# Unused bytes between the halves of the weights' tiles in a gated mix of linear attention and a gated unit

## The chip, the cores and the metric

The kernel runs on one core of one Trainium2 chip. The metric is the time of one execution in device microseconds (us), the median of several runs. Beside it there is one execution recorded by the hardware profiler, and all views of the profile are of that one.

## The reference

An input `x` of 2048 tokens by 640 goes through two branches, and a gate per token mixes them. Everything is float32.

```python
g = _sigmoid((x * gate_w).sum(-1, keepdims=True))
# a: linear attention, 32 heads of 20
qkv = (x @ wqkv) ...                       # q, k, v: 2048 x 640 each
phi = lambda t: jnp.where(t > 0, t + 1, jnp.exp(t)) + 1e-6
kv  = einsum("bhsd,bhse->bhde", phi(k), v);  z = einsum("bhsd->bhd", phi(k))
num = einsum("bhqd,bhde->bhqe", phi(q), kv); den = einsum("bhqd,bhd->bhq", phi(q), z) + 1e-6
a   = (num / den) @ wo
# b: gated unit, F = 1536
h = _sigmoid(x @ w_gate) * (x @ w_up)
b = h @ w_down
return g * a + (1 - g) * b
```

## The kernel before

**Precision.** Every large product is made of three matmuls (`mm3`, lines 189 to 193). Each operand is split by ScalarE and VectorE into a high part and a low part, both float32r (`split`, line 219). `mm3` issues high by high (L190), weights' high by the streamed low part (L191), and weights' low by the streamed high part (L192). So the weights loaded into TensorE go high, high, low, and each matmul loads its own 128 x 128 weights. Nearly all matmuls after the first phase stream 512 columns.

**Stages.** First K and the state (sum over tokens of phi(K) and x): 320 and 322 columns wide, tiles of many sizes. Then the tokens go in two passes of 1024: `pr` = 1, then `pr` = 0. A pass has a Q projection (`q_phase`), twelve blocks of the gated unit (`f_phase`, class `Block`) with the down-projection woven in, and `last_down`. At the end, the output stage multiplies the scaled phi(Q), `pq`, by a combined matrix held in `ws` and `wf` tiles and mixes.

**A block.** `Block.s1` to `s7` form the gate and the up product of 128 features together, with seven products in place of eight (sums of tiles are formed first). In terms, a term being one `mm3`: `s1` and `s2` use five of `wg`; `s4` one and `s6` three of `wu`; `s3`, `s4`, `s5` and `s7` two, two, two and three of `ws`. That is 18 terms, 54 matmuls. What is streamed are the forms of `x`: tiles `xa`, `xr`, `xb`, `xt`, with h or l for the part. A Q projection unit takes 15 matmuls with `wg`; of its streamed tiles those for the first two chunks of the second half are `b12`.

**Weights.** In the first pass a weights' tile is made by splitting (`wg_split`, `queue_s`) and stored to DRAM by GpSimd's queue (`store_w`, line 800). In the second pass SyncE's queue loads it back (`load_form`, line 871), two blocks ahead, into the buffer that the block before last has just left. The tiles are `wg` (two halves of 640), `wu` (two of 384) and `ws` (two of 1152 floats per partition), two buffers each; half 0 is the high part, half 1 the low part. A `wg` tile also holds the last two down weights of the second pass (`load_wd`). One `ws` and one `wu` tile serve the output stage as plain room (`load_m`, `load_p`).

**Where tiles lie.** Pools are stacked from two sides of SBUF. On the right, from the top downward: `px` (the `x` forms, later `pl` and `pq`), `pg` (`wg`), `pw` (from its bottom upward: `t`, `wu`, `ws`, `c`). All these tiles have sizes that are multiples of 256 bytes, and in the program's allocation all of them start at 224 modulo 256: `wg` at bytes 153,568 and 158,688, `wu` at 118,752 and 121,824, `ws` at 124,896 and 134,112, the `x` forms from 163,808 on. On the left lie `hf` (the products h), `wd` and `wf` (down weights): 47,456, 79,200 and 63,840, all at 96 modulo 256. At the very bottom of SBUF there are 16,384 bytes per partition that GpSimd's DMA uses as scratch. In the first phase tiles have sizes such as 2,576 and 1,288 bytes and lie at all multiples of 32 modulo 256.

**Order.** `Order` plans in program order when ScalarE's and VectorE's side work is issued between matmuls, from estimated durations; each engine and queue then runs its own list in order.

Of the kernel before, what the change touches and what calls it, by code (L numbers as in the profile page):

```python
# [8 lines left out]
F32R = mybir.dt.float32r  # L9
# [6 lines left out]
P = 128  # L16
S, D, F = 2048, 640, 1536
# [3 lines left out]
TG = 512  # L21
# [146 lines left out]
def gated_mix_kernel(ctx: ExitStack, tc: tile.TileContext, xt, xn, wk, wv, wo, wst_q, wst_f, out_t):  # L168
    nc = tc.nc
# [7 lines left out]
    def f32(ap):  # L177
        return ap.bitcast(F32)
# [40 lines left out]
    def split(hi, lo, src, after=""):  # L219
        act(hi, src, AF.Copy, after)  # L220
        at = order.act

        def low():
            order.vec = max(order.vec, at)
            vec2(lo, src, f32(hi), OP.subtract)
        order.then(low)
# [37 lines left out]
    def m1_tile(tag, name, dt=F32, rows=P):  # L264
        return m1.tile([rows, D], dt, name=name, tag=tag, bufs=2)
# [114 lines left out]
    def queue_forms(nx):  # L380

        nx[0].queue_a()
        nx[0].queue_b()
        order.add(0, 0, lambda: nx[1].load(((0, 0, 2), (0, 2, KC), (1, 2, KC), (1, 0, 2))))
        nx[1].queue_a()
        nx[1].queue_b()
        nx[1].queue_sums()
        order.add(0, 0, lambda: nx[0].load(((1, 2, 4), (0, 0, 2), (1, 0, 2), (0, 2, 4))))
        nx[0].queue_sums()
# [67 lines left out]
    def queue_ks():  # L457
        for s, sums in ((1, (0, 2, 1)), (0, ()), (2, ()), (3, (3,))):
            for j in range(2):
                for t in sums:  # L460
                    order.add(0, v_cost(HW), lambda t=t, j=j: k_sum(t, j))
            for j in range(2):
                order.add(a_cost(HW), v_cost(HW), lambda s=s, j=j: k_form(s, j), ("ks", s))
        order.add(a_cost(HW), 2 * v_cost(HW), k_fifth_d, ("ks", 5))
# [4 lines left out]
    def tok(b, side):  # L469

        pr, j = divmod(b, 4)
        return (2 * pr + side) * 4 + j
# [14 lines left out]
    def queue_xn(b):  # L487
        for n in (2 * b, 2 * b + 1):
            order.add(a_cost(D), v_cost(D), lambda n=n: split_xn(n), ("xn", b), lambda n=n: xn_st[n][1])
# [115 lines left out]
    def k_split(i, after=""):  # L605
        r = KR[i]
        ph, pl = op_tile("pkh"), op_tile("pkl")
        vh, vl = (t[:, :D].rearrange(view2, j=2) for t in (ph, pl))
        act(vh, r, AF.Copy, after, bias=EPS)
        at = order.act  # L610

        def low():
            order.vec = max(order.vec, at)
            vec3(vl, r, EPS, f32(vh), OP.add, OP.subtract)
        order.then(low)
        PK[i] = (ph, pl)
# [12 lines left out]
    def queue_split(b):  # L629
        for s in range(2):  # L630
            order.add(a_cost(D), v_cost(D), lambda s=s: k_split(tok(b, s)), ("pk", b))

    def queue_z(b):
        for s in range(2):
            order.add(0, v_cost(D), lambda s=s: z_add(tok(b, s)), ("z", b))
# [84 lines left out]
    g = GTBatch(0, [0])  # L720
# [8 lines left out]
    for c in range(1, 4):  # L729
        ck = chunks[c]  # L730
        if c == 1:
            a, b = KPlain(2), KPlain(3)
            order.need((ck, "plain"))
            queue_ks()
            queue_xn(2)
            order.need(("z", 0))
            for k in range(KC):
                a.k(k)
                order.fill()
            order.need(("z", 1))  # L740
            a.phi_a()
            for k in range(KC):
                b.k(k)
                order.fill()
                if k == 0:
                    a.phi_b()
                    order.add(0, 0.6, constants)
            order.need(("ks", 5))
            for t in range(2):
                k_split(tok(2, t))  # L750
        else:
            a, b = KBlock(2 * c), KBlock(2 * c + 1)
            for n in range(1, 6):
                order.need((ck, n))
                if c == 2 and n >= 3:
                    order.need(("ks", (1, 0, 2)[n - 3]))
                getattr(a, f"s{n}")()
                getattr(b, f"s{n}")()
                if n == 2:
                    queue_xn(2 * c)  # L760
            order.need((ck, 6))
            if c == 2:
                order.need(("ks", 5))
            if c + 1 < len(chunks):
                chunks[c + 1].load()
            else:
                nx = [Chunk(1, i, None, i * CW, xst_v, (b12h, b12l)) for i in range(2)]
                nx[0].load()
            a.s6()
            a.s7()  # L770
            order.need(("z", 2 * c - 1))
            a.sum_b()
            a.phi_a()
            b.s6()
            a.phi_b()
            order.need(("pk", 2 * c - 1))
            k_split(tok(2 * c, 0))
            b.s7()
            b.sum_b()
            k_split(tok(2 * c, 1))  # L780
        if c == 3:
            pa_cm.__exit__(None, None, None)
            px_cm = tc.tile_pool(name="px", bufs=1, side="right", reuse_waits="tile")
            px = px_cm.__enter__()
            xf = XForms(px, TG)
            pg_cm = tc.tile_pool(name="pg", bufs=1, side="right", reuse_waits="tile")
            pg = pg_cm.__enter__()
            W, WT = {}, {}

            def wg_tile():  # L790
                return pg.tile([P, 2, D], F32R, name="wg", tag="wg", bufs=2)

            def put(n, i, t):
                WT[n, i] = t
                W[n, i] = [t[:, c] for c in range(2)]

            def store_w(n, i):

                w_dram[n[2], i] = dram.tile(list(WT[n, i].shape), F32, name=f"w{n[2]}{i}")
                nc.gpsimd.dma_start(w_dram[n[2], i], f32(WT[n, i]))  # L800

            def wg_split(n, src):
                put(n, 0, wg_tile())
                split(*W[n, 0], src)
                if n[0] == "f":
                    order.then(lambda: store_w(n, 0))
            nx[0].f = nx[1].f = xf
        elif c == 1:
            chunks[2].load()
        g = GTBatch(c, batches[c])  # L810
        order.need(("xn", 2 * c))
        queue_z(2 * c)
        if c < 3:
            chunks[c + 1].queue()
        else:
            queue_xn(7)
        for u in range(4):
            g.part(u, 0, 2, ("rot", "dd", "ch", "cc")[u])
            if u == 0:
                order.need(("z", 2 * c))  # L820
                b.phi_a()
            if u == 1:
                b.phi_b()
        queue_split(2 * c + 1)
        queue_z(2 * c + 1)
        if c < 3:
            queue_xn(2 * c + 1)
        else:
            w_stage = [m1_tile("ma", "w0") for _ in range(2)]
            for n in range(2):  # L830
                nc.sync.dma_start(w_stage[n], wst_q[:, n])
            queue_forms(nx)
        for u in range(2 * KC):
            g.part(u, 2 if u < 4 else 0, 4)
            order.fill()
# [17 lines left out]
    pw = pw_cm.__enter__()  # L853
# [7 lines left out]
        return pw.tile(list(shape), dt, name=name, tag="c", bufs=5)  # L861

    def wu_tile():
        return pw.tile([P, 2, 3 * P], F32R, name="wu", tag="wu", bufs=2)

    def ws_tile():
        return pw.tile([P, 2, 9 * P], F32R, name="ws", tag="ws", bufs=2)

    def load_form(n, i):
        t = (wg_tile, wu_tile, ws_tile)[i]()  # L870
# [820 lines left out]
    PL, PQ, BL, OMG, MHL = {}, {}, {}, {}, {}  # L1691
# [7 lines left out]
    def load_m(i):  # L1699

        n = (0, 3, 10)
        t = (ws_tile, wf_tile)[i]().rearrange("p a b -> p (a b)")[:, :(n[i + 1] - n[i]) * D]
        nc.sync.dma_start(f32(t), mp_dram.rearrange("p a b c -> p (a b c)")[:, n[i] * D:n[i + 1] * D])
        for j in range(n[i], n[i + 1]):
            MHL[divmod(j, 2)] = t[:, (j - n[i]) * D:(j - n[i] + 1) * D]

    def load_p(g):

        n = groups.index(g)
        if n == 0:  # L1710
            PL[g] = [tt("pl") for _ in range(KC - 1)]
            PL[g].append(f32(wu_tile()).rearrange("p a b -> p (a b)")[:, :TG])
            for u in range(KC):
                nc.sync.dma_start(PL[g][u], p_dram[:, u, g])
        else:
            PL[g] = []
            for u in range(0, KC, 2):
                t = (x2_tile if n % 2 else h_tile)(dt=F32)
                w = min(2, KC - u)
                nc.sync.dma_start(t[:, :w], p_dram[:, u:u + w, g])  # L1720
                PL[g] += [t[:, i] for i in range(w)]
        PL[g, "at"] = order.pe + 6.0
# [137 lines left out]
```

## Time and profile before

| | |
|---|---|
| median of 3 runs | 758.25 us (757.82 to 758.86) |
| profiled execution | 760.14 us; span 758.4 us from first to last instruction |
| granted clock of TensorE | 0.999 |
| busy | TensorE 750.9 us in 3,699 matmuls, VectorE 558.3, ScalarE 309.1, GpSimd 72.9 |
| DMA | 155.27 MB, mean 205 GB/s |

The span leaves out what lies around the first and last instruction, so the profiled execution's own time stands beside it. In the rows, `PE` is TensorE's matmuls and `PEld` its weight loads, `DVE` VectorE, `ACT` ScalarE, `POOL` GpSimd, `SPq` SyncE's queue. A row of a group has the line, engine and operation, the tiles (written <- read, or for matmuls: written <- streamed, weights), the shape, the count, and then the busy time in us and the mean duration of one in ns. A row of the timeline has start and duration in us. A matmul's duration is longer than the distance to the next start, since matmuls are pipelined; differences of durations, and distances between starts, are what can be compared. A row of windows gives, for a stretch, busy us and count of each engine, the granted clock, the busy share of the DMA engines and GB/s. A row of DMA issues gives count, KB each and the median us from issue to landing.

### The profile page before, as it was taken

The page shows a single profiled execution, that of the slowest core. Times are in us where ns is not written, and L with a number is a line of the kernel's source. Part 1 is how long each engine was busy: PE and PEld are TensorE (multiplying, and loading weights), DVE is VectorE, ACT ScalarE, POOL GpSimd, SP SyncE. Part 2 cuts the span into 40 slices and gives each one's busy share as a digit, 9 for nine tenths or more (in the row PEclk, how much of TensorE's full clock was granted, in tenths as well). Part 3 has the DMA queues.
Part 4 walks back from the last instruction along what each step waited for, and adds up shares of the span by engine and source line. Part 5 has one row for each costly group of instructions (what it writes and reads, how often), then busy time and mean ns, then how long its engine had stood idle before and what let it go on. Part 6 is the DMA issues. An engine that isn't in the chain of part 4 may idle for free.

```text
span 758.4 us, 10012 instructions
## 1 busy us (share of the span) xinstructions
PE 750.9 (99%) x3699; PEld 642.3 (85%) x3699; DVE 558.3 (74%) x978; ACT 309.1 (41%) x578; POOL 72.9 (10%) x131
## 2 busy tenths in 40 slices
PE   9999999999999999999999999999999999999998
PEld 7999999988878888888888888788888888887886
DVE  4988778876586677877888865575868776886863
ACT  5673546366465634343444454353222313221110
POOL 0000000023122422121121210000000000000000
PEclk9999999999999999999999999999999999999999
DMA  7230414597987797566475744956363636277243
GB/s 260 67 109 1 140 39 135 181 276 263 334 320 267 276 380 277 207 255 241 190 258 220 288 164 148 381 200 237 124 243 132 241 119 243 91 270 257 105 139 111
DMA packets 57110, 155.27 MB, mean 205 GB/s; under 512 B 9303, under 2 KB 20823, under 8 KB 53861
## 3 DMA queue, kind: packets, MB, share of 16 engines
q1 hardware_dynamic: 44933, 99.31, 38.9%
q0 software_dynamic: 12128, 55.32, 18.8%
q8 instruction: 29, 0.48, 0.3%
q14 instruction: 20, 0.16, 0.1%
HBM read 97.33 MB, written 60.56 MB: 208 GB/s over the span
## 4 chain that ended last, share of the span: by engine, by line
PE 88%; DMA 5%; issue 2%; DVE 2%; ACT 1%; POOL 1%; SPq 1%; POOLq 0%; ACTq 0%; DVEq 0%
PE dd L192 8%; PE dd L190 8%; PE dd L191 8%; PE ch L190 8%; PE ch L192 8%; PE ch L191 8%; PE rot L191 7%; PE rot L192 7%; PE rot L190 7%; PE cc L192 6%; PE cc L190 6%; PE cc L191 6%; DMA wst<-wst_f 2%; DMA pden<-p_dram 2%; DMA wv_sb<-wv 1%
## 5 line engine op out<-in xcount | busy, mean ns | idle before, releaser
L202 ACT ACTIVATE c<-ch 128x512 f32<-128x512 f32 x72 | 43.0, 597 | 157.3 <-PE ch L192 155.6
L206 DVE TENSOR_TENSOR hf<-c,hf 128x512 fp32r<-128x512 f32 x63 | 43.2, 688 | 27.0 <-ACT hf L202 26.4
L206 DVE TENSOR_TENSOR tb<-dd,tb 128x512 f32<-128x512 f32 x75 | 51.1, 687 | 15.0 <-PE dd L192 14.6
L206 DVE TENSOR_TENSOR c<-cc,c 128x512 f32<-128x512 f32 x48 | 32.9, 685 | 29.6 <-ACT c L202 22.6
L202 ACT ACTIVATE c<-c 128x512 f32<-128x512 f32 x48 | 30.1, 628 | 49.8 <-DVE c L206 49.8
L206 DVE TENSOR_TENSOR tb<-rot,tb 128x512 f32<-128x512 f32 x64 | 43.5, 687 | 6.2 <-PE rot L192 5.8
L202 ACT ACTIVATE hf<-c 128x512 fp32r<-128x512 f32 x63 | 39.3, 625 | 18.8 <-DVE c L206 18.5
L190 PE MATMUL dd<-xrh,wg 128*128 128x512 f32 x102 | 40.0, 392 | 0.0
L191 PE MATMUL dd<-xrl,wg 128*128 128x512 f32 x102 | 39.8, 390 | 0.0
L192 PE MATMUL dd<-xrh,wg 128*128 128x512 f32 x102 | 39.7, 390 | 0.0
L190 PE MATMUL ch<-xth,ws 128*128 128x512 f32 x96 | 37.5, 390 | 1.2 <-ACT c L202 1.2
L192 PE MATMUL ch<-xth,ws 128*128 128x512 f32 x96 | 37.5, 391 | 0.0
L191 PE MATMUL ch<-xtl,ws 128*128 128x512 f32 x96 | 37.4, 389 | 0.0
L190 PE MATMUL rot<-pkh,xnh 128*128 128x320 f32 x102 | 31.6, 310 | 0.0
L191 PE MATMUL rot<-pkl,xnh 128*128 128x320 f32 x102 | 31.6, 309 | 0.0
L192 PE MATMUL rot<-pkh,xnl 128*128 128x320 f32 x102 | 31.4, 308 | 0.0
L206 DVE TENSOR_TENSOR c<-c,c 128x512 f32<-128x512 f32 x44 | 30.2, 686 | 1.4 <-ACT c L202 0.9
L1016 POOL DMA_DIRECT2D p_dram<-qr x20 | 11.1, 555 | 205.7 <-DVE qr L210 198.5
L192 PE MATMUL cc<-xbh,ws 128*128 128x512 f32 x72 | 28.0, 389 | 0.0
L190 PE MATMUL cc<-xbh,ws 128*128 128x512 f32 x72 | 28.0, 389 | 0.0
L191 PE MATMUL cc<-xbl,ws 128*128 128x512 f32 x72 | 28.0, 389 | 0.0
L202 ACT ACTIVATE pq<-pl 128x512 fp32r<-128x512 f32 x14 | 8.5, 630 | 40.3 <-DVE pl L210 40.3
(474 smaller groups left out, 2300.9 us busy)
## 6 DMA issues: line engine op xcount, KB each, us to landing
w<-ws POOLq DMA_DIRECT2D x12, 1152.0 KB, 7.1
ws<-w SPq DMA_DIRECT2D x12, 1152.0 KB, 8.5
wst<-wst_f SPq DMA_DIRECT2D x12, 640.0 KB, 5.5
w<-wg POOLq DMA_DIRECT2D x12, 640.0 KB, 4.8
wd<-wd POOLq DMA_DIRECT2D x12, 640.0 KB, 6.5
wg<-w SPq DMA_DIRECT2D x12, 640.0 KB, 4.2
xst<-xt SPq DMA_DIRECT2D x10, 640.0 KB, 6.5
wf<-wd SPq DMA_DIRECT2D x10, 640.0 KB, 5.5
```

The lines of the kernel that those rows point to most:

```text
L190: nc.tensor.matmul(out, l_hi, r_hi, start=first, stop=False, skip_group_check=True)
L191: nc.tensor.matmul(out, l_hi, r_lo, start=False, stop=False, skip_group_check=True)
L192: nc.tensor.matmul(out, l_lo, r_hi, start=False, stop=last, skip_group_check=True)
L202: nc.scalar.activation(out, src, fn, **kw)
L206: nc.vector.tensor_tensor(out, a, b, op=op)
L1016: nc.gpsimd.dma_start(p_dram[:, u, g], r)
```

## The change

Each half of a weights' tile gets unused bytes behind it: 96 for `wg`, 32 for `wu`, 64 for `ws`. The tile that the rest of the program sees is cut back to the old width, so no matmul, split or transfer changes its amount of data; in SBUF a tile that was one run per partition becomes two. The two places that use a tile as plain room take the whole of it. The scratch of GpSimd's DMA is set to 8,192 bytes per partition.

```diff
             def wg_tile():
-                return pg.tile([P, 2, D], F32R, name="wg", tag="wg", bufs=2)
+                return pg.tile([P, 2, D + 24], F32R, name="wg", tag="wg", bufs=2)[:, :, :D]
...
     def wu_tile():
-        return pw.tile([P, 2, 3 * P], F32R, name="wu", tag="wu", bufs=2)
+        return wu_whole()[:, :, :3 * P]
+
+    def wu_whole():
+        return pw.tile([P, 2, 3 * P + 8], F32R, name="wu", tag="wu", bufs=2)
 
     def ws_tile():
-        return pw.tile([P, 2, 9 * P], F32R, name="ws", tag="ws", bufs=2)
+        return ws_whole()[:, :, :9 * P]
+
+    def ws_whole():
+        return pw.tile([P, 2, 9 * P + 16], F32R, name="ws", tag="ws", bufs=2)
...
-        t = (ws_tile, wf_tile)[i]().rearrange("p a b -> p (a b)")[:, :(n[i + 1] - n[i]) * D]
+        t = (ws_whole, wf_tile)[i]().rearrange("p a b -> p (a b)")[:, :(n[i + 1] - n[i]) * D]
...
-            PL[g].append(f32(wu_tile()).rearrange("p a b -> p (a b)")[:, :TG])
+            PL[g].append(f32(wu_whole()).rearrange("p a b -> p (a b)")[:, :TG])
...
-    nc = bacc.Bacc("TRN2", target_bir_lowering=False, num_devices=1)
+    nc = bacc.Bacc("TRN2", target_bir_lowering=False, num_devices=1, dynamic_dma_scratch_size=8192)
```

## The prediction

> **What bounds the kernel now.** I read the page first: busy times, slices, then the view of waits for TensorE alone.
>
> ```profile
> span 758.4 us, 10012 instructions
> ...
> PE 750.9 (99%) x3699; PEld 642.3 (85%) x3699; DVE 558.3 (74%) x978; ACT 309.1 (41%) x578; POOL 72.9 (10%) x131
> ...
> PE   9999999999999999999999999999999999999998
> ...
> PEclk9999999999999999999999999999999999999999
> ```
>
> ```profile
> PE ch L190 <- ACT c L202: 1.2, 1, 1.2
> PE ch L190 <- DVE c L206: 0.6, 1, 0.6
> PE rot L191 <- DVE pq L206: 0.4, 1, 0.4
> ```
>
> TensorE is busy in every slice, at the full granted clock, and in the middle of the kernel it waits 2.2 us for anybody. So nothing that the other engines or the queues gain can be worth more than about 2 us, and the change adds no matmul and removes none. Only one thing can move the end by more: the distance in time from one matmul's start to the next one's, which I call the pitch. It is not one number. The next rows are from the timeline of TensorE; each pair is the first and the last matmul of a stretch with no wait in it, and the times are starts.
>
> A stretch of 53 matmuls in the first pass over F (weights in `ws`, `wu`, `wg`, streamed data in the `x` forms; both at offset 224 modulo 256):
>
> ```profile
> 213.31 0.39 PE L192 MATMUL ch<-xth,ws 128*128 128x512 f32 x1
> ...
> 225.12 0.39 PE L190 MATMUL ch<-xth,ws 128*128 128x512 f32 x1
> ```
>
> 52 steps in 11.81 us: 227.1 ns. Next, 57 matmuls of the last down-projection, whose weights `wd` were loaded into `wg` tiles (offset 224) while the streamed `hf` is on the left side (offset 96):
>
> ```profile
> 670.76 0.39 PE L190 MATMUL rot<-hf,wg 128*128 128x512 f32 x1
> ...
> 683.83 0.39 PE L192 MATMUL rot<-hf,wg 128*128 128x512 f32 x1
> ```
>
> 56 steps in 13.07 us: 233.4 ns. And the output stage, where the streamed `pq` is at 224 and the weights are at 224 for one and a half of five terms and at 96 for the others; 228 steps lie between the two rows:
>
> ```profile
> 695.25 0.39 PE L190 MATMUL ch<-pq,ws 128*128 128x512 f32 x1
> ...
> 748.24 0.39 PE L190 MATMUL cc<-pq,ws 128*128 128x512 f32 x1
> ```
>
> 52.99 us by 228 gives 232.4 ns. The same instruction, at the same clock, with no wait recorded, takes 5.3 to 6.3 ns longer where weights and streamed data lie differently. The groups say the same of durations, for one and the same streamed tile `hf`, with weights at its own offset and 128 bytes from it:
>
> ```profile
> L190 PE MATMUL dd<-hf,wf 128*128 128x512 f32 x50 | 19.6, 391 | 0.0
> ```
>
> ```profile
> L190 PE MATMUL dd<-hf,wg 128*128 128x512 f32 x8 | 3.2, 396 | 0.0
> ```
>
> My reading: while one matmul streams, the weights of the next are read, and the two reads disturb each other by an amount that depends on their offsets. Equal offsets, repeated matmul after matmul, settle into a steady beat of 227 ns; anything else never settles.
>
> **The change, part by part.** Where do the weights come to lie? Every tile of the right side has a size that is a multiple of 256 bytes, so all of them now share 224. After the change a `wg` half is 96 bytes past a multiple of 256 and its tile 192, a `wu` half 32 and its tile 64, a `ws` half 64 and its tile 128. Stacked in the same order this gives, for high and low half: `wg` 96 and 192 in one buffer, 32 and 128 in the other; `wu` 224 and 0, 32 and 64; `ws` 96 and 160, 224 and 32. The pools of `x` forms lie above them and stay at 224, and 8 KB less of scratch at the bottom moves the left side by a multiple of 256. So the weights spread, what they are multiplied with does not, and the steady beat of equal offsets ends for these tiles. `hf` with `wd` and `wf` stays as it is.
>
> How many matmuls is that? The three rows are TensorE's matmuls that read `wg`, then `ws`, then `wu`:
>
> ```profile
> 0.00:758.40 758.40, 171.76 (x750) 1.00 0.58 205
> ```
>
> ```profile
> 0.00:758.40 758.40, 182.97 (x753) 1.00 0.58 205
> ```
>
> ```profile
> 0.00:758.40 758.40, 73.29 (x288) 1.00 0.58 205
> ```
>
> 1,791 in all. Of these 60 stream `hf`, 90 stream `b12` and 105 stream `pq`; those are either off the beat already or (70 of them) 256 columns wide. 1,536 are left: 24 blocks of 54 and 240 of the Q projection, all 512 wide and now at 227.1.
>
> What will they cost? In half of the `wu` and `ws` buffers the high half stays at 224, and two of three matmuls of a term read it: 24 blocks by 13 terms by a half by 2 are 312 matmuls. The nearest rows for equal offsets off the beat are those of `pq` with `ws`, in the window from 705 to 750 us; ahead of them the page's row of `ws` on the beat:
>
> ```profile
> L190 PE MATMUL ch<-xth,ws 128*128 128x512 f32 x96 | 37.5, 390 | 1.2 <-ACT c L202 1.2
> ```
>
> ```profile
> L191 PE MATMUL ch<-pq,ws 128*128 128x512 f32 x6 | 2.4, 396 | 0.0
> ...
> L190 PE MATMUL ch<-pq,ws 128*128 128x512 f32 x6 | 2.3, 389 | 0.0
> ...
> L192 PE MATMUL ch<-pq,ws 128*128 128x512 f32 x3 | 1.2, 393 | 0.0
> ```
>
> Their mean is 393 where the beat has 390: 3 ns, times 312 is 0.9 us. The other 1,224 get the mean of the two stretches off the beat, 232.9 less 227.1 or 5.8 ns: 7.1 us. Sum for TensorE: 8.0 us.
>
> No stretch shows 512 columns at distances other than 0 and 128, so I bound this from both sides. Narrow matmuls are the other end: in the first phase tiles have sizes such as 2,576 bytes and lie at all multiples of 32.
>
> ```profile
> 50.23 0.31 PE L190 MATMUL rot<-pkh,xnh 128*128 128x320 f32 x1
> ...
> 59.49 0.30 PE L190 MATMUL rot<-pkh,xnh 128*128 128x320 f32 x1
> ```
>
> ```profile
> 428.29 0.28 PE L190 MATMUL rot<-b12h,wg 128*128 128x256 f32 x1
> ...
> 429.60 0.28 PE L192 MATMUL rot<-b12h,wg 128*128 128x256 f32 x1
> ```
>
> ```profile
> 751.03 0.28 PE L190 MATMUL ch<-pq,ws 128*128 128x256 f32 x1
> ...
> 754.46 0.28 PE L192 MATMUL ch<-pq,wf 128*128 128x256 f32 x1
> ```
>
> 63 steps give 147.0 ns at 320 columns and mixed offsets; 11 steps give 119.1 at 256 and equal offsets; 29 steps give 118.3 at 256 and mixed ones. From 119.1 at 256 and 227.1 at 512, equal offsets would have 146.1 at 320. So mixing costs +0.9 ns at 320 and -0.8 at 256: over 1,536 matmuls +1.4 or -1.2 us. The upper end is 6.3 ns for all 1,536, 9.7 us. I take the rows of 512 columns because they are the same instruction; that the loss shows only there fits a disturbance that goes on after the weights are in.
>
> The Trainium skill (TensorE: Matmul & The Clock Gate, Step-by-step: what each phase is for) has TensorE read streamed data and weights through two independent ports, so that loading the next weights takes nothing from the running matmul. By that rule the offsets would be worth 0 us; the rows of 227.1 and 233.4 ns do not agree with it.
>
> The transfers: each weights tile is now two runs per partition in SBUF. GpSimd's issue and the landings of tiles that already go in two runs (`wd`) stand beside those in one:
>
> ```profile
> L1235 POOL DMA_DIRECT2D wd<-wd x12 | 8.2, 684 | 24.6 <-DVE wd L206 21.9 <-DVE c L206 2.2 <-issue 0.2
> ...
> L800 POOL DMA_DIRECT2D w<-wg x12 | 6.5, 545 | 34.1 <-DVE wg L206 34.1
> ```
>
> ```profile
> ws<-w SPq DMA_DIRECT2D x12, 1152.0 KB, 8.5
> ...
> w<-wg POOLq DMA_DIRECT2D x12, 640.0 KB, 4.8
> wd<-wd POOLq DMA_DIRECT2D x12, 640.0 KB, 6.5
> ...
> wg<-w SPq DMA_DIRECT2D x12, 640.0 KB, 4.2
> ...
> wg<-wd SPq DMA_DIRECT2D x2, 640.0 KB, 6.6
> ```
>
> 36 stores by 139 ns are 5 us of GpSimd, spread over the first pass, and it idles before them, waiting for VectorE. A landing may grow by 1.7 to 2.4 us. In the second pass a block's `ws` load, the largest, is issued when the block two before it ends: the 54 matmuls of the block between, 12.3 us at 227.1 ns, cover its 8.5 us and 2 more. So this stays hidden; if that cover were gone, a block would wait for what of the landing is over 12.3 us. But in two places TensorE does wait for a landing:
>
> ```profile
> 194.75 14.67 DMA wst<-wst_f
> ...
> 477.36 12.17 DMA pden<-p_dram
> ```
>
> ```profile
> 200.00:215.00 15.00, 13.81 (x61) 11.08 (x61) 8.76 (x16) 7.38 (x13) 2.30 (x4) 1.00 0.82 332
> ...
> 470.00:495.00 25.00, 24.36 (x107) 19.83 (x107) 15.95 (x24) 8.36 (x15) 0.54 (x1) 1.00 0.90 336
> ```
>
> There it idles 1.2 and 0.6 us with the DMA engines 82 and 90% busy and weights' transfers among the traffic. I add 0.3 us, between -0.5 (a slower TensorE before them eats part of the wait) and 3 (both landings later by 1.5). The scratch of 8 KB changes nothing that TensorE waits for: no row shows GpSimd waiting for it, 0 us.
>
> Sum: 8.0 + 0.3 = 8.3 us. The profiled execution took 760.14 us (span 758.4 and 1.7 around it), 1.9 over the median of the runs; it would take 768.4. On the median of 758.25 that is 766.5 us.
>
> **The rivals.** (1) The forecast, slower by 4 to 13 us: chance 0.72; with 0.05 for a loss between 1.5 and 4 us (part of the steps find a beat again) and 0.03 for more than 13. (2) No difference: the mixing costs what the rows of 320 columns say, +1.4 us with transfers hidden, 759.7. For it speaks that one rate per column joins 256, 320 and 512 columns; against it the two stretches at 512. 0.09. (The port rule of the Trainium skill's page TensorE: Matmul & The Clock Gate belongs to this case.) (3) Not slower but faster: spread offsets let some terms dodge the disturbance altogether, as the 118.3 against 119.1 ns at 256 columns hints. At -0.8 ns over 1,536 matmuls it gives 757.0, and it decides for the kernel from a mean pitch under 226.1 ns. Against it: no stretch of 512 columns shows a mean below 227. 0.11.
>
> **The numbers.** About 0.2%, 1.5 us, is what a measurement of this kernel can tell from no change. Case 1 with its neighbours gives slower 0.80, case 2 same 0.09, case 3 faster 0.11. The range runs from case 3's 757.0 to 758.25 + 9.7 + 3, 771.0.
>
> **What would show it.** Right: in the changed kernel's timeline, blocks of `ws`, `wu`, `wg` have a mean pitch near 232 ns, group means move from 390 to about 395, `hf` with `wf` stays at 391, TensorE's waits stay at some 2 us, and the span grows evenly through both passes over F, by about 0.28 us per block (6.75 us of the 8.0 over 24 blocks). Wrong: a pitch still at 227 (then the offsets of equal value were not the cause of the beat), a pitch below it, or a growth that sits in the windows from 200 to 215 and 470 to 495 us, which would make it the transfers.

## The result, and the profile after

The changed kernel takes 764.36 us (median of 4 runs, 763.67 to 765.46) against 758.21 for the kernel before in the same comparison. The ratio is 1.0079, with a 95% interval of 1.0065 to 1.0094: 6.15 us slower. The forecast was 766.5, 8.3 us slower, so the sign and most of the size were right and the size was a third too large.

The page of the changed kernel's profile; the profiled execution took 763.74 us:

```profile
span 762.0 us, 10010 instructions
...
PE 756.5 (99%) x3699; PEld 642.0 (84%) x3699; DVE 558.7 (73%) x978; ACT 309.2 (41%) x578; POOL 77.7 (10%) x131
...
PEclk9999999999999999999999999999999999999999
```

TensorE is busy 5.6 us longer with the same 3,699 matmuls at the same clock. The timeline shows where. These are the same first and last matmul of the two stretches that the prediction measured, first 53 matmuls of `ws`, `wu` and `wg`, then 57 of `hf` with down weights in `wg` tiles:

```profile
211.78 0.40 PE L192 MATMUL ch<-xth,ws 128*128 128x512 f32 x1
...
223.82 0.39 PE L190 MATMUL ch<-xth,ws 128*128 128x512 f32 x1
...
674.49 0.40 PE L190 MATMUL rot<-hf,wg 128*128 128x512 f32 x1
...
687.44 0.39 PE L192 MATMUL rot<-hf,wg 128*128 128x512 f32 x1
```

52 steps in 12.04 us are 231.5 ns (227.1 before); 56 steps in 12.95 us are 231.3 ns (233.4 before). The first stretch has lost its beat. The second never had one, and has got another loss in place of the old one. Over all 512-column matmuls that stream an `x` form (1,523 and 1,527 distances between starts; distances above 300 ns, which hold waits, are left out) the mean pitch went from 227.4 to 231.8 ns, 6.7 us in all. The loss lies in both passes: the window from 215 to 330 us holds 502 matmuls instead of 509, the one from 495 to 600 us 456 instead of 462.

The waits of TensorE went the other way. The view of its waits, whole, and the windows in which the prediction looked for the transfers:

```profile
PE rot L279 <- POOL warm L276: 1.4, 1, 1.4
PE rot L191 <- DVE pq L206: 0.4, 1, 0.4
```

```profile
200.00:215.00 15.00, 15.00 (x66) 12.20 (x65) 11.13 (x21) 8.76 (x16) 2.70 (x4) 1.00 0.96 384
...
470.00:495.00 25.00, 25.00 (x109) 20.18 (x108) 15.47 (x23) 7.96 (x14) 0.54 (x1) 1.00 0.90 319
```

Both waits for landings (1.2 and 0.6 us before) are gone. GpSimd's stores and the landings, in the groups and in the DMA issues:

```profile
L800 POOL DMA_DIRECT2D w<-wg x12 | 8.2, 679 | 31.9 <-DVE wg L206 31.9
```

```profile
ws<-w SPq DMA_DIRECT2D x12, 1152.0 KB, 8.1
...
w<-wg POOLq DMA_DIRECT2D x12, 640.0 KB, 4.9
...
wg<-w SPq DMA_DIRECT2D x12, 640.0 KB, 4.5
```

A store's issue takes 679 ns instead of 545, and GpSimd is busy 4.8 us longer, which nobody waits for. These landings moved by -0.4, +0.1 and +0.3 us, not by the 1.7 to 2.4 that was allowed for.

### The profile page after: what moved, and what is told of

It is laid out like the page before. It is cut to its first block, busy times and chain, and to the rows that moved or that the text cites. A ratio compares the mean times of both kernels' runs of the same rounds, so it can differ in the third digit from the quotient of the medians.

```text
span 762.0 us, 10010 instructions
## 1 busy us (share of the span) xinstructions
PE 756.5 (99%) x3699; PEld 642.0 (84%) x3699; DVE 558.7 (73%) x978; ACT 309.2 (41%) x578; POOL 77.7 (10%) x131
## 4 chain that ended last, share of the span: by engine, by line
PE 99%; DVE 0%; POOL 0%; issue 0%; POOLq 0%
PE dd L191 9%; PE dd L190 9%; PE dd L192 9%; PE ch L190 9%; PE ch L191 9%; PE ch L192 9%; PE rot L191 8%; PE rot L190 8%; PE rot L192 8%; PE cc L190 7%; PE cc L192 7%; PE cc L191 7%; PE ch L1186 1%; PE rot L279 1%; PE rot L1082 0%; DVE tb L206 0%
## 5 line engine op out<-in xcount | busy, mean ns | idle before, releaser
L190 PE MATMUL dd<-xrh,wg 128*128 128x512 f32 x102 | 40.4, 396 | 0.0
L190 PE MATMUL ch<-xth,ws 128*128 128x512 f32 x96 | 37.6, 392 | 0.0
L190 PE MATMUL rot<-pkh,xnh 128*128 128x320 f32 x102 | 31.5, 309 | 0.0
L190 PE MATMUL cc<-xbh,ws 128*128 128x512 f32 x72 | 28.2, 391 | 0.0
```

Of the source, the lines that this page charges most:

```text
L190: nc.tensor.matmul(out, l_hi, r_hi, start=first, stop=False, skip_group_check=True)
```

## Experiments

Theory A says that the distance modulo 256 bytes between a matmul's streamed data and the weights that are loaded meanwhile sets the pitch. Its rivals are the transfers in two runs (B), the scratch (C), the jump between the halves (D), the place of the weights by itself (E) and traffic of other engines (F); G, H and I are named where they were tested.

**The scratch alone.**

```diff
-    nc = bacc.Bacc("TRN2", target_bir_lowering=False, num_devices=1)
+    nc = bacc.Bacc("TRN2", target_bir_lowering=False, num_devices=1, dynamic_dma_scratch_size=8192)
```

> The kernel before with the scratch of GpSimd's DMA at 8 KB and nothing else; every tile keeps its offset modulo 256. Theory A (the distance modulo 256 bytes between a matmul's weights and the data streamed beside their load sets the pitch): no difference, 758.2 us. Rival B (the new layout of the transfers, tiles of two runs): no difference either, 758.2. Rival C (the smaller scratch makes GpSimd's issues or its transfers slower): the whole or a part of the 6.2 us, up to 764.4.

Measured: ratio 1.0012 (0.9999 to 1.0025), 758.9 us. This is the program of before with its left side 8,192 bytes lower, so its profile is nearly a second execution of that kernel, and a wait that it does not show need not belong to the program. Its waits and the window of the first one:

```profile
PE rot L279 <- POOL warm L276: 1.4, 1, 1.4
PE ch L190 <- DVE c L206: 0.9, 1, 0.9
PE rot L191 <- DVE pq L206: 0.4, 1, 0.4
```

```profile
200.00:215.00 15.00, 15.00 (x67) 12.40 (x67) 10.87 (x20) 8.78 (x16) 2.30 (x4) 1.00 0.98 389
```

The wait near 210 us does not recur here; the one near 488 us does. Rival C would need 6 us to explain the change and has at most 1.9.

**Unused bytes, but in multiples of 256.**

```diff
-                return pg.tile([P, 2, D + 24], F32R, name="wg", tag="wg", bufs=2)[:, :, :D]
+                return pg.tile([P, 2, D + 64], F32R, name="wg", tag="wg", bufs=2)[:, :, :D]
...
-        return pw.tile([P, 2, 3 * P + 8], F32R, name="wu", tag="wu", bufs=2)
+        return pw.tile([P, 2, 3 * P + 64], F32R, name="wu", tag="wu", bufs=2)
...
-        return pw.tile([P, 2, 9 * P + 16], F32R, name="ws", tag="ws", bufs=2)
+        return pw.tile([P, 2, 9 * P + 64], F32R, name="ws", tag="ws", bufs=2)
```

> The changed kernel with 256 unused bytes behind every half instead of 96, 32 and 64: the tiles are again two runs per partition, their transfers and GpSimd's issues as in the changed kernel, but both halves of all weights lie at 224 modulo 256, as what they are multiplied with. Theory A: the steady beat returns, TensorE busy 751 us, 758.2 us, and the two waits for landings (1.2 and 0.6 us) return in some form; 758 to 759.5. Rival B (transfers of two runs): stays at 764.4, or at least 760. Rival C (scratch): 764.4 as well.

Measured: ratio 1.0012 (1.0003 to 1.0022), 759.37 us. From its page and its groups:

```profile
PE 750.4 (99%) x3699; PEld 642.2 (85%) x3699; DVE 558.8 (74%) x978; ACT 309.2 (41%) x578; POOL 77.5 (10%) x131
```

```profile
L800 POOL DMA_DIRECT2D w<-wg x12 | 8.2, 679 | 31.2 <-DVE wg L206 31.2
```

Everything that the change does to transfers is here (679 ns per store, GpSimd at 77.5), and TensorE is back at 750.4 us. Of the two waits one is back, with 1.0 us near 488 us; none is near 210 us. So the two-run transfers and the scratch together are worth 0.2 to 1.7 us at the most, and the offsets the rest. Rival B falls.

**All weights 128 bytes away, in one run each.** This kernel and the later ones are made from the kernel before, and set the scratch to 8,192 bytes as well, where the text says nothing else; that line is left out of the diffs.

```diff
+            px.tile([P, 32], F32, name="gap")
             xf = XForms(px, TG)
```

> The kernel before with one unused block of 128 bytes below the x forms (and the scratch of 8 KB): wg, wu and ws keep one run each, but all of them lie at 96 modulo 256 where the x forms stay at 224, a constant distance of 128. Theory A: the 1,536 matmuls lose the beat, 232.4 to 233.4 ns instead of 227.3, 7.8 to 9.3 us of TensorE; off it come 0.3 us for hf with wg, whose offsets become equal, and up to 2 us of waits that a slower TensorE takes in: 764 to 767 us, at least as slow as the changed kernel. Rival B: 758.2, for the transfers are as before. Rival D (it is the jump between the high and the low half at different offsets that costs): 758.2, for the two halves lie at the same offset.

Measured: ratio 1.0104 (1.0091 to 1.0117), 766.3 us, slower than the changed kernel. The same two stretches in its timeline:

```profile
212.64 0.40 PE L192 MATMUL ch<-xth,ws 128*128 128x512 f32 x1
...
224.73 0.39 PE L190 MATMUL ch<-xth,ws 128*128 128x512 f32 x1
...
676.69 0.40 PE L190 MATMUL rot<-hf,wg 128*128 128x512 f32 x1
...
689.40 0.39 PE L192 MATMUL rot<-hf,wg 128*128 128x512 f32 x1
```

12.09 us by 52 are 232.5 ns where both halves lie at the same offset, and the transfers are those of before: rival D falls. And 12.71 us by 56 are 227.0 ns for `hf` with `wg`, which one and the same block of 128 bytes has put at equal offsets.

**The left side 128 bytes higher.** Here equality is extended to what never had it: `hf`, `wd`, `wf` and `b12` come to 224.

```diff
+    common.tile([P, 32], F32, name="gap")
     e_mat = common.tile([P, P], F32R, name="e_mat")
```

> The kernel before with one unused block of 128 bytes at the bottom of the left side (and the scratch of 8 KB): hf, wd, wf and b12 move from 96 to 224, so the offsets of weights and streamed data become equal also in the last down-projection, for b12 and in the output stage. Theory A: the 379 matmuls of 512 columns that were 128 bytes apart go from 233.0 to 227.3 ns, 2.1 us less: 756.1 us; the first phase, whose left tiles move by 128 bytes against its right ones, can take or give up to 1 us (755 to 757). Rivals B, C and D: 758.2.

Measured: ratio 0.9964 (0.9948 to 0.9980), 755.79 us. It beats both kernels. Its page, and the last down-projection and the output stage in its timeline:

```profile
PE 747.7 (99%) x3699; PEld 642.5 (85%) x3699; DVE 558.0 (74%) x978; ACT 308.9 (41%) x578; POOL 72.9 (10%) x131
```

```profile
667.83 0.39 PE L190 MATMUL rot<-hf,wg 128*128 128x512 f32 x1
...
680.52 0.39 PE L192 MATMUL rot<-hf,wg 128*128 128x512 f32 x1
...
691.73 0.39 PE L190 MATMUL ch<-pq,ws 128*128 128x512 f32 x1
...
743.41 0.39 PE L190 MATMUL cc<-pq,ws 128*128 128x512 f32 x1
```

12.69 us by 56 and 51.68 us by 228: 226.6 and 226.7 ns, where the kernel before had 233.4 and 232.4. TensorE's busy time falls by 3.2 us. Of that the output stage (283 matmuls of 512 columns, 232.5 to 227.1 ns) gives 1.6, and `hf` with `wf` (270, 228.4 to 226.7) and with `wg` (60, 233.2 to 226.7) 0.5 and 0.4; the `x` forms, 227.4 to 227.0 ns, most of the rest.

**The same with the scratch left at 16 KB.** The diff is the one line above.

> The kernel before with the one unused block of 128 bytes at the bottom of the left side and nothing else; the scratch stays at 16 KB. Theory A: as with the small scratch, 755.8 us (755 to 756.8), faster than the kernel before and than the changed one. Rival C (part of that gain came from the scratch): 757 or more.

Measured: ratio 0.9973 (0.9957 to 0.9988), 756.8 us; in that comparison the kernel before had 759.1. The gain of 2.3 us is, within the intervals, the 2.5 us that the same line brought with the small scratch; the time itself is at the upper end of theory A's range and 0.2 us below that of rival C. So the one line gains time without the scratch; a small part for the scratch is not excluded.

**The pitch by itself.** A kernel in which TensorE runs 103 blocks of 36 matmuls, high, high, low, on data that lies still.

```python
for s, a, b, n in plan():      # offsets in steps of 32 bytes: streamed, weights high, weights low; columns
    mv = xs[:, 0, int(s * 8):int(s * 8) + n]
    w = [xs[:, 1, int(o * 8):int(o * 8) + P] for o in (a, b)]
    for i in range(N):         # N = 36
        nc.tensor.matmul(ps[k // 15 % 4][:, :n], w[i % 3 == 2], mv, ...)
        k += 1
```

> TensorE alone: 103 blocks of 36 matmuls in the order high, high, low, with nothing beside them; the rest of the computation is left out and the output is not the reference's. Streamed data at 224 modulo 256; weights' high and low part at all 64 pairs of offsets in steps of 32 bytes (512 columns), then constant distances in half steps (16 bytes more), equal offsets at the seven other places, and 320 and 256 columns at the eight constant distances; the constant distances of 512 columns once more at the end. Theory A (the distance alone counts): equal offsets 226.7 ns wherever they lie; high and low both 128 bytes away 233.5; the pairs that the changed kernel has (high and low at 128 and 224, 64 and 160, 0 and 32, 64 and 96, 128 and 192, 0 and 64 bytes past the streamed data) 229 to 233, and their mean within 1 ns of the 231.8 that the changed kernel shows off the beat. Rival D (jumps between the halves cost): constant distances all 226.7, mixed pairs above. Rival E (the offset of the weights itself counts, not the distance): equal offsets at other places than 224 come out at 229 to 233. Rival F (it is other engines' traffic in SBUF that the offsets meet): with nothing else running all blocks come out at 226.7. At 320 columns 146.7 and at 256 118 to 119.5, whatever the distance.

Three stretches of its timeline; a row is the matmuls that wrote one tile, so the distance of two starts is 15 pitches. First both halves 160 bytes past the streamed data, then 192, then equal:

```profile
389.91 3.66 PE L54 MATMUL ch<-xs 128*128 128x512 f32 x15
393.41 3.66 PE L54 MATMUL dd<-xs 128*128 128x512 f32 x15
...
759.07 3.60 PE L54 MATMUL rot<-xs 128*128 128x512 f32 x15
762.50 3.62 PE L54 MATMUL ch<-xs 128*128 128x512 f32 x15
...
807.97 3.56 PE L54 MATMUL dd<-xs 128*128 128x512 f32 x15
811.37 3.56 PE L54 MATMUL cc<-xs 128*128 128x512 f32 x15
```

3.50, 3.43 and 3.40 us by 15 are 233.3, 228.7 and 226.7 ns. All 64 pairs of distances, in ns, each the mean of 27 distances within a block (the first is from the last block of the run, since the first matmuls of the first block were still 427 ns apart):

```
low part:      0      32     64     96     128    160    192    224   bytes past the streamed data
high   0     226.7  233.4  231.1  232.6  231.3  233.3  231.4  231.1
      32     231.9  233.3  231.3  232.3  231.5  233.4  232.6  231.0
      64     231.1  235.5  233.3  231.1  231.1  232.4  231.9  232.9
      96     230.1  235.5  232.4  234.4  231.6  231.1  233.4  233.2
     128     233.3  231.1  229.9  233.1  232.4  233.3  233.3  232.1
     160     231.1  233.3  231.1  231.1  233.3  233.4  233.3  231.1
     192     228.8  229.7  233.2  229.1  231.0  233.3  228.9  230.9
     224     233.3  231.3  231.1  233.3  231.1  231.7  232.4  233.3
```

This kernel ran once. The seven unequal constant distances were run again at its end and came out within 0.1 ns of the table, but for 128 bytes with 233.1 instead of 232.4. Equal offsets gave 226.7 to 226.9 ns at the seven other places too, so for them the place does not matter and rival E falls; unequal ones were taken with the streamed data at 224 alone. (For 128 bytes the full kernel has a second place: 233.2 ns for `hf` at 96 with `wg` at 224, 232.8 for the `x` forms at 224 with weights at 96.) Other engines were idle, so rival F falls; rival D falls again, since constant unequal distances lose as well. No pair reaches 226.7 but the equal one. At 320 columns seven of the eight distances gave 146.7 ns and the eighth 146.6; at 256, where 118 to 119.5 was expected, equal offsets were the slowest, 120.0, the others 117.4 to 119.9. Equal offsets thus lie on one line, 120.0, 146.7 and 226.7 ns at 256, 320 and 512 columns: 0.417 ns per column and 13.3 ns on top. The six pairs that the changed kernel holds are 128 with 224 (232.1), 64 with 160 (232.4), 0 with 32 (233.4), 64 with 96 (231.1), 128 with 192 (233.3) and 0 with 64 (231.1); two of them are just above the 229 to 233 that were expected, and their mean is 232.2.

**A cheaper distance in the full kernel: 192 bytes.** The diff is that of the 128 bytes with `[P, 16]`.

> As the kernel with all weights 128 bytes from the x forms, but with 64 unused bytes instead of 128, so that wg, wu and ws lie at 160 where the x forms stay at 224: a constant distance of 192. In the table of pitches this is the cheapest unequal distance, 228.9 ns against 226.7 for equal and 233 for 128. Theory A with the table: 1,527 matmuls by 2.2 ns, 3.4 us of TensorE, less 0.3 for pq with ws and up to 0.8 of the wait near 488 us: 760.5 to 761.5 us. Rival G (every unequal distance costs the same in the full kernel, since other traffic blurs what the table shows): 765 to 766.5 as at 128.

Measured: ratio 1.0045 (1.0030 to 1.0061), 762.47 us against 759.11, 3.4 us slower. That is 1.0 us above the range, of which 0.8 is the kernel before, which took 758.31 in the earlier comparisons. The first of the two stretches in its timeline:

```profile
212.78 0.39 PE L192 MATMUL ch<-xth,ws 128*128 128x512 f32 x1
...
224.68 0.40 PE L190 MATMUL ch<-xth,ws 128*128 128x512 f32 x1
```

11.90 us by 52 are 228.8 ns, and by the table 228.9; over all `x` forms it is 229.65. It lost 3.4 us where 128 bytes lost 8.0, so the full kernel follows the table, and rival G falls.

**240 unused bytes, meant as a distance of 16.** The same diff with `[P, 60]`.

> The same with 240 unused bytes, so that wg, wu and ws begin 16 bytes past the x forms modulo 256. Theory A as the table has it (units of 32 bytes count; 226.7 ns at 16 bytes past): no difference, 758.3 us. Rival H (equal to the byte is needed): 764 to 766 us.

Measured: ratio 1.0001 (0.9988 to 1.0014), 758.84 us, with 227.4 ns for the `x` forms: no loss. But the 16 bytes did not come about. In this program's allocation the block takes 256 bytes, and `wg` begins at 153,312 and 158,432, `wu` at 118,496 and 121,568, `ws` at 124,640 and 133,856: all at 224 modulo 256, as before. So this is one more control that moves the weights by 256 bytes, and rival H was not tested in the full kernel. The table alone bears on it, in its half steps: with the weights 16 bytes past the streamed data the pitch is 226.7 ns, as for equal offsets, and with 16 bytes short of it (240 past) 228.3. So equal need not mean equal to the byte, but the two sides are not alike.

**One part of the change: `wg` alone.** The block `gap` keeps `wu` and `ws` at 224.

```diff
+            pg.tile([P, 32], F32, name="gap")
             W, WT = {}, {}
...
-                return pg.tile([P, 2, D], F32R, name="wg", tag="wg", bufs=2)
+                return pg.tile([P, 2, D + 24], F32R, name="wg", tag="wg", bufs=2)[:, :, :D]
```

> One part of the change alone: 96 unused bytes behind the halves of wg, at 96 and 192 in one buffer and 32 and 128 in the other as in the changed kernel; wu and ws stay whole and at 224. Theory A: 591 matmuls by 4.5 ns (232.2 less 227.7), 2.7 us, less up to 0.8 of the wait near 488 us: 760.1 to 761.0 us; ws stays at 227.1 ns, wu at 227.4. Rival I (a spread anywhere breaks the beat of the matmuls around it as well): 762 or more, with ws and wu above 229 ns.

Measured: 761.22 us, just above the range; ratio 1.0022 (1.0008 to 1.0037), which is 1.7 us (0.6 to 2.8). Matmuls with `wg` had 232.1 ns, those with `ws` 227.1 and with `wu` 228.2. Two groups from its profile, one of each kind:

```profile
L190 PE MATMUL dd<-xrh,wg 128*128 128x512 f32 x102 | 40.4, 396 | 0.0
...
L190 PE MATMUL ch<-xth,ws 128*128 128x512 f32 x96 | 37.4, 389 | 0.0
```

`xrh` with `wg` is at the changed kernel's 396, `xth` with `ws` at 389, as in the kernel with the scratch alone. The beat is lost tile by tile and found again within the next product; rival I falls, but for 0.8 ns on `wu`.

## Why the prediction was right, and where its size was off

**What bounds the kernel, and the reading of the offsets: right.** The kernels that only move tiles by some bytes show it both ways: 8.0 us lost at 128 bytes and 3.4 at 192, 2.5 gained where the left side is made equal, nothing lost where the weights move by 256 (ratio 1.0001), and at most 1.7 us where the unused bytes come in multiples of 256. That the offset between streamed data and weights sets the pitch is shown. That the loss comes from the read of the next weights beside the running stream fits this but is argued; what it is that collides stays open. The Trainium skill (TensorE: Matmul & The Clock Gate, Step-by-step: what each phase is for) lets the two operands come through independent read ports, so that loading the next weights takes no read bandwidth from the running matmul; the table, taken with every other engine idle, does not agree with it: 226.7 ns against up to 235.5 by the distance alone.

**Which matmuls: right.** 1,536 were counted, 1,527 distances measured, and `hf` with `wd` stayed at 227.0 ns. The output stage, which the count left out, moved both ways: `pq` with `ws` went from 230.5 to 232.6 ns (93 distances) and with `wf` from 233.5 to 232.5 (190), 0.2 us each, which cancel.

**The cost of each: the term that was mis-sized.** The prediction took 5.8 ns for 1,224 matmuls, from the two stretches at 233.4 and 232.4, and 3 ns for 312 at equal offsets among unequal ones. Measured, by the offset of the weights of the matmul that follows: 4.5 ns (231.9 less 227.4) for 1,229 and 3.9 (231.3) for 298, so 6.7 us instead of 8.0. Two things explain it. The stretches of before, wholly or mostly at 128 bytes, had 232.9, and the table has 232.4 and 233.1 for that distance; the six pairs of the change average 232.2 there. That none of them is one of the cheap pairs, as 192 with 192 (228.9), was luck: the prediction had no row for any distance but 0 and 128. And a part of the weights gets off cheaper in the full kernel than alone: `wg` and `wu` are at 232.2 and 232.1 as the table has them, `ws` at 231.2. Why `ws` gains 1 ns is not settled. The rows at 320 and 256 columns, taken as the lower bound, are no smaller version of the same effect: alone, 320 columns show no dependence on the distance at all, and the 147.0 of the first phase is 0.3 ns from the 146.7 of equal offsets, not 0.9.

**The transfers: right that they are hidden; the sign of the small term stays open.** The prediction added 0.3 us. The landings grew by less than it allowed. The wait near 488 us is 0.6 us in the profile of the kernel before, 0.9 and 1.0 in two controls (the scratch alone, multiples of 256), and gone in the changed kernel. That a slower TensorE takes it in, as the prediction's lower end for this term (-0.5) has it, fits these four but is not shown, for the wait differs between executions: it is 0.1 us in the kernel with 240 unused bytes, whose TensorE is as fast as before, and 1.3 with `wg` alone, whose TensorE is slower. 6.7 for the `x` forms, 0.2 for `hf`, and some 0.8 us less of this wait would make 6.1, where the medians differ by 6.15; that they agree so closely is in part luck.

**What would show it.** Pitch of a block 231.5 against "near 232": right. `ch<-xth,ws` on L190 went to 392 and `dd<-xrh,wg` to 396, where "about 395" was forecast. `hf` with `wf` moved from 391 to 392 (L190), 228.4 to 229.5 ns, which was to stay; why is open. That waits stay at some 2 us was wrong. Of these, the 1.2 us near 210 us belong to some executions only: two of the nine later profiles of the full kernel show such a wait there (0.4 and 2.0 us), and the profiled execution of before had been 1.9 us above the median. The view of waits of one execution cannot tell that.

**The rivals.** No difference (759.7) and faster (757.0) both rested on narrow matmuls, and both are ruled out by the interval. The faster one decided below a mean pitch of 226.1 ns; in the table nothing at 512 columns lies below 226.7.

## What to carry to other kernels

Where TensorE never waits, measure the distance between the starts of its matmuls, not their durations, and group it by tiles; a group that is 5 ns slower than another of the same shape may only lie elsewhere. For 512 float32r columns and new weights at every matmul, weights and streamed data at the same offset modulo 256 bytes had 226.7 ns and all other pairs in steps of 32 bytes 228.8 to 235.5, so spreading the tiles is the wrong way, and one unused block of 128 bytes on the other side was worth 2.5 us here. A variant that moves tiles by multiples of 256 bytes is the control that separates offsets from everything else an edit does. And look up in the allocation where a tile has come to lie: 240 unused bytes moved the weights by 256.

## What was not expected

The loss need not grow with the number of unequal matmuls: with only one weight tile of three off, at 32 bytes, the table has 233.4 ns, as much as with all three off. A beat needs the whole term.

And in one execution a wait cost nearly twice its length. In the profiled execution of the kernel with the left side moved and 16 KB of scratch, which took 759.5 us where the median is 756.8, TensorE waits 2.0 us near 211 us. Its timeline, then windows:

```profile
210.53 0.39 PE L192 MATMUL cc<-xbh,wu 128*128 128x512 f32 x1
212.94 0.50 PE L190 MATMUL ch<-xth,ws 128*128 128x512 f32 x1 [2.02 <-ACT c L202]
...
213.66 0.63 PE L192 MATMUL ch<-xth,ws 128*128 128x512 f32 x1
...
216.65 0.44 PE L190 MATMUL ch<-xah,wg 128*128 128x512 f32 x1
```

```profile
212.00:216.00 4.00, 3.06 (x8) 2.45 (x9) 3.90 (x8) 2.43 (x5) 1.75 (x3) 0.66 0.68 270
```

The granted clock fell to 0.66 in this window. Between the last two rows of the timeline lie seven steps: 2.99 us, 427 ns each, 1.4 us more than at 227. The 1.2 us wait of the kernel before left the clock at 1.00. The Trainium skill (TensorE: Matmul & The Clock Gate, Part 1: The HAM clock gate) gives 426.7 ns at 512 columns for the half clock, with which this row agrees; it names an idle window of some 3.4 us for the fall, and here the fall came with a wait of 2.0 us.
